# Decode out of the mLSTM loop, other PSUM banks, low parts on POOL, and a last tile in token order

## The chip, the cores and the metric

One core of one Trainium2 chip runs the whole program in one launch. The metric is device time in microseconds (us), the median of several runs. The engines are TensorE (PE, its weight loads as PEld), VectorE (DVE), ScalarE (ACT), GpSimd (POOL) and SyncE (SP, which issues most DMAs). DMA engines move data between HBM and SBUF; matmuls write to PSUM, which has eight banks here called `bk[0]` to `bk[7]`.

## The reference

Three layers follow one another, all with float32 results. The first is an mLSTM over 4 batches, 8 heads, 768 steps of width 40:

```
m_new = maximum(f[t] + m, i[t]);  fs = exp(f[t] + m - m_new);  is = exp(i[t] - m_new)
C = fs * C + is * outer(v[t], k[t]);   n = fs * n + is * k[t]
y[t] = sigmoid(o[t]) * (C @ q[t]) / maximum(abs(n . q[t]), 1)
```

Its result, 3072 tokens of width 320, goes to a mixture of 8 experts: `logits = x @ w_gate + modality_bias[modality]`, each token goes to the one expert with the largest logit, and gets `gate * (relu(x @ w1[e]) @ w2[e])`, where `gate` is the softmax weight of that expert and the inner width is 1024. The last layer is dense with inner width 2048: `h = x @ w_in; out = (h * cos(h)) @ w_out`.

## The kernel before, in words

All instructions stand in an order written out by hand (`manual_schedule`); each engine runs its own in that order and waits on semaphores for the others. A PSUM bank is one tile.

**mLSTM loop.** `for i in range(NT)`, 24 iterations; iteration i handles 128 steps (chunk c = i // 4) of batch i % 4. It issues `exps(i+1)` (ACT exponentials L427, POOL selections L436, POOL products), `scores(i)` (TensorE L466 and L474, VectorE products L480), `values(i-1)` (TensorE L493 into bank 6, L500, L508; VectorE L517 to L544; POOL division L546), loads for i+3 on SP, `spread_later(i+2)`, `logits(i-3)` (TensorE L570, VectorE L571) and `xpose(i-2)` (TensorE L557 into bank 2, ACT L559). Small VectorE work waits in a list `bg` of generators; `fill(n)` issues n of its operations at marked places, `drain()` all.

**Routing.** Every four iterations `route` chooses the expert of each token, and `rank_mm(c)` (L666 to L677) with `rank` (L692 on) counts its place among its expert's tokens; for chunks 0 to 3 the counts go to bank 6 (columns 64 on), for 4 to bank 7, for 5 to bank 4. `cnt` (L687) copies the totals after 16 and 20 iterations. `pick_first`, `early_slot` and `early_rows` choose the experts of slot 0 and 1 and find their rows with matmuls L815, whose result goes to bank 7 (slot 0) or bank 5; `gather` (L857, indirect DMA on POOL) then brings 256 rows of the tokens written so far into XS.

**Decode.** `w_in` and `w_out` of the last layer come as 64-bit words and are turned into float32 by `_decode`, 20 pieces of 128x512 or 128x640: ACT L1760, VectorE L1761, L1767, L1771, L1775, in four steps. Three pieces (`PIECES[:DA]`) are done in the mLSTM loop, two steps at the end of each iteration with i % 4 < 2 from 4 to 17, with loads on SP; the other 17 in slots 2 to 10, a step for each block, with loads on ACT's queue.

**Experts.** Tokens sorted by expert fill slots of 256 rows, s = 0 to 11, and seven shorter ones. A slot has 8 blocks f: `ffn1` (L976, 8 matmuls), `relu` (ACT L982 and VectorE L983, which makes the low part), `ffn2` of block f-2 (L997, 6 matmuls). Float32 precision comes from high and low parts: a weight is copied to a high part by ACT (L936, L945), and VectorE or POOL subtracts (`sub`, L927) to get the low part: `split_in(r1, f, d, eng, eng2)` for w1, `split_out` for w2. `xpose_b` makes the slot's input the same way (TensorE L877, ACT L881, VectorE L882). Ahead of slot 0, `first_slot` issues rank 4, then 14 operations of `bg`, then the low parts of blocks 1 and 2, then `xpose_b(0)`. `finish` scatters each result row to its place in `x2_d` (indirect DMA, index `cinv`), which `compact` computes so that unused rows are skipped; the row's number in the output is stored in its first column.

**Cosine stage.** 6 tiles of 512 rows of `x2_d`; 16 blocks each (`c_ffn1` L1651, `c_phase`, `c_cos`, `c_split`, `c_ffn2` L1683). The output rows are copied out of PSUM by VectorE (L1690) or ACT (L1692) in groups of 128 and scattered by POOL (L1003) to the rows given by `ids`.

Of the kernel before, what the change touches and what calls it, by code (L numbers as in the profile page):

```python
# [34 lines left out]
NTAB = NS + NU  # L35
EARLY = (16, 20)
DV = D + 1
MAGIC = 12582912.0
# [4 lines left out]
DU3 = 3  # L43
DA = 3
STEPS = (2, 2)

# [49 lines left out]
def kernel(  # L96
# [101 lines left out]

    F0 = 3

# [186 lines left out]
    Mc = many(ge2, B, "Mc", NP, DV)  # L387
    raw_t = [ge2.tile([128, 640, 2], U32, name=f"raw{i}") for i in range(2)]
    dtu_t = [ge2.tile([128, 640], U32, name=f"dtu{i}") for i in range(2)]
    for t_ in M[0:2]:  # L390
# [270 lines left out]
    def rank_mm(c):  # L661
        j0, n = c * B, B
        r = slice(j0, j0 + n)
        b_ = bk[(6, 7, 4)[max(c - NC + 3, 0)]]
        pk = b_[:, 64:64 + n * E]
        T_.matmul(out=pk, lhsT=trib[:, 0, :], rhs=oh[:, r].rearrange("p j e -> p (j e)"), start=True, stop=False)  # L666
        pk3 = pk.rearrange("p (j e) -> p j e", j=n)
        for j in range(n - 1):
            T_.matmul(
                out=pk3[:, j + 1:], lhsT=trib[:, 1, :],  # L670
                rhs=oh[:, j0 + j].unsqueeze(1).to_broadcast([128, n - 1 - j, E]), start=False, stop=False,
            )
# [9 lines left out]
    def rank_first(c, pk3):  # L682

        g = rank(c, pk3)
        next(g)
        if (c + 1) * B in EARLY:
            V.tensor_copy(out=cnt, in_=bk[6 if c < NC - 2 else 7][:, 128:128 + E])  # L687
        return g
# [151 lines left out]
    def early_rows(k):  # L840
        pv = bk[5 if k else 7][:, 0:4]
        slot_mm(k, EARLY[k], pv)
        with nc.allow_low_precision("whole numbers"):
            V.tensor_reduce(
                out=inv[:, 2 * k:2 * k + 2].unsqueeze(2), in_=pv.rearrange("p (a h) -> p h a", a=2), axis=AX.X,
                op=ALU.add,
            )
# [168 lines left out]
    def bstep(s, f):  # L1016
# [17 lines left out]
        if s > 2 or f > 1:  # L1034
            next(dec[0], None)
        if f == 4 and s + 1 < NS:
            fl[s + 1] = flag_regs(tab[s + 1:s + 2, 1:2])
# [24 lines left out]
    def weigh_later(c):  # L1062
        if c < SLOW:
            wt[c] = weights(c)
            bg.append(wt[c])
            return
        run(weights(c))
        wq.append(weigh(c))
        wt[c] = in_turn(rank_first(c, rank_mm(c)), rows_of(c))
        bg.append(wt[c])  # L1070

    dec_ops = _decode(nc, (raw_t, dtu_t), w_in, w_out, w_ir, None, PIECES[:DA])
    exps(0)
# [11 lines left out]
    for i in range(NT):  # L1085
# [8 lines left out]
        else:  # L1094
            exps(i + 1)
            if i >= 4 and i < NT - 1 and (i - 4) % B == B - 1 and (i - 4) // B >= SLOW:
                ex_exp((i - 4) // B)
            scores(i)
        if i == NT - 2:
            run(e0)  # L1100
            early_rows(0)
            gather(0)
        if i >= 1:
            values(i - 1)
# [27 lines left out]
        if i >= 3:  # L1132
            logits(i - 3)
        if i >= 2:
            xpose(i - 2)
        if i >= 8 and i % B == 0 and i // B - 2 < SLOW:
            c = i // B - 2
            bg.append(in_turn(rank_first(c, rank_mm(c)), rows_of(c)))
        if i >= 3 and (i - 3) % B == B - 1:
# [4 lines left out]
        if i >= 4 and i < NT - 1 and (i - 4) % B == B - 1:  # L1144
# [4 lines left out]
            weigh_later(c)  # L1149
            if i == EARLY[0] + 3:  # L1150
                pf = pick_first()
                bg.append(pf)
        if i >= 8 and i % B == 0 and i // B - 2 < SLOW:
# [7 lines left out]
        if i == EARLY[0] + 4:  # L1161
            load_w(0, 0)
        if i == 2:
            next(dec_ops)
        if B <= i < EARLY[0] + 2 and i % B < 2:
            for _ in range(STEPS[i % 2]):
                next(dec_ops, None)
        if i == NT - 2:
            for _ in dec_ops:
                pass  # L1170
            pe_.close()
# [7 lines left out]
    ex_exp(NC - 2)  # L1179
    split_in(w1r, 0, 0, G_, G_)  # L1180
    for f in (1, 2):
        split_in(w1r, f, f, V, V, (0,))
    run(weights(NC - 2))
# [5 lines left out]
    def first_slot():  # L1189
        rk_ = rank_first(NC - 2, rank_mm(NC - 2))  # L1190
        bg.extend([in_turn(pick_second(), early_slot(1, sc)), in_turn(rk_, rows_of(NC - 2))])
        fill(14)
        for f in (1, 2):
            split_in(w1r, f, f, V, V, (1,))
        for _ in xpose_b(0, (4, 1, 0)):
            fill(F0)
        for _ in range(2):
            next(we)
        split_out(w2r, 0, 0, V)

# [3 lines left out]
    split_in(w1r, 3, 3, V, V)  # L1204
    split_out(w2r, 1, 1, V)
    pl_.close()
# [71 lines left out]

    iv, pvs = small("iv", NL), small("pvs", NL)

    def slot_index():
# [4 lines left out]
        yield  # L1286
        V.scalar_tensor_tensor(out=inv[:, 4:], in0=pvs, scalar=-1.0, in1=iv, op0=ALU.add, op1=ALU.add)
        yield
# [37 lines left out]
    G_.memset(val[:, 0:4], 1.0)  # L1326
    pc = bk[3][:, 0:NH]

    def compact():
# [4 lines left out]
        yield  # L1334
        V.tensor_scalar(out=runs, in0=runs, scalar1=cst[:, C_P:C_P + 1], scalar2=4096.0, op0=ALU.add, op1=ALU.add)
        yield
        V.scalar_tensor_tensor(out=cinv, in0=val, scalar=-4096.0, in1=runs, op0=ALU.mult, op1=ALU.add)
        yield
# [23 lines left out]
    for k in range(2 * NF):  # L1362
        s, f = divmod(k, NF)
        ffn1(s, f)
        if k == 7:
            next(xgs[1])
        fill(2 if k in (0, 7) else 5)
        relu(s, f)
        if k == 7:
            next(xgs[1])  # L1370
        if k == 2:
            logits(NT - 2)
            xpose(NT - 1)
# [36 lines left out]
        if k == 5:  # L1410
            drain()
            we = weigh(NC - 1)
            bg += [halves()]
        if k >= 5:
# [7 lines left out]
        if NF - 3 <= k < 2 * NF - 3:  # L1422
            new_weights(1, k - NF + 3)
        if k == 8:
            drain()
# [4 lines left out]
        if k == 11:  # L1430
            drain()
            load_w(2, 0)
            V.tensor_scalar(out=val[:, 4:], in0=pvs, scalar1=0.0, scalar2=None, op0=ALU.is_gt)
        if k == 12:
            load_w(2, 1)
        if k == 13:
            T_.matmul(out=pc, lhsT=trib[:, 1, :], rhs=val, start=True, stop=True)
            bg += [compact(), out_rows()]
            xgs[2] = xpose_b(2)
# [25 lines left out]
    dtu_b = [rb.tile([128, 640], U32, name=f"dtu{i}") for i in range(2)]  # L1465
    dec[0] = _decode(nc, (raw_b, dtu_b), w_in, w_out, w_ir, w_or, PIECES[DA:], A)
    next(dec[0])
# [13 lines left out]
    def xpose_c(T, xs, xh, xl, banks):  # L1481
        G_.tensor_copy(out=ids[:, 4 * T:4 * T + 4], in_=xs[:, :, 3].bitcast(I32))
        A.activation(out=xs[:, :, 4 + DM:], in_=xs[:, :, 4 + 256:4 + DM], func=AF.Copy)
# [191 lines left out]
    def c_ffn2(T, *fs):  # L1675
        for j in range(TT):
# [10 lines left out]
            if fs[-1] == NFC - 1:  # L1687
# [3 lines left out]
                else:  # L1691
                    A.activation(out=os_, in_=po, func=AF.Copy)  # L1692
                scatter(out[:, :], ids[:, T * TT + j:T * TT + j + 1], os_, "out")

# [156 lines left out]
```

## Time and profile before

| what | value |
|---|---|
| median of 3 runs | 748.97 us (747.42 to 749.36) |
| profiled execution | 745.15 us, span 743.5 us, 16872 instructions |
| PE busy | 705.6 us (95%), 6132 matmuls |
| DVE busy | 527.9 us (71%) |
| ACT busy | 386.8 us (52%) |
| POOL busy | 214.9 us (29%) |
| HBM read, written | 84.58 MB, 12.14 MB |

The profile is taken from one execution; its time is the span plus what lies around it. Busy times are shares of the whole span, while the stages have different limits, so they are read by stretches. Matmul ends are modelled, so a busy PE is not PE at its peak.

### The profile page before, as it was taken

To read this page: it belongs to the slowest core of one execution; us is meant where nothing else is said; L and a number is where in the kernel's file an instruction comes from. 1 tells how busy PE (TensorE), PEld (TensorE's weight loads), DVE (VectorE), ACT (ScalarE), POOL (GpSimd) and SP (SyncE) were. 2 spreads that over 40 slices of the span, in tenths; PEclk is the share of its full clock that TensorE was granted. 3 is DMA by queue.
4 is the path that set the end of the run, shared out by engine and by line. 5 is a ranking of instruction groups with operands and counts; after the bars stand their busy time and mean duration, and the time that the engine had idled before them with its cause. 6 is when DMAs were issued, how large, how long until landed. Compare 5 with 4: busy or idle time off the path is not lost. (4 is left out here: it accounts for less than half of the span.)

```text
span 743.5 us, 16872 instructions
## 1 busy us (share of the span) xinstructions
PE 705.6 (95%) x6132; PEld 650.3 (87%) x6132; DVE 527.9 (71%) x1208; ACT 386.8 (52%) x910; POOL 214.9 (29%) x282
## 2 busy tenths in 40 slices
PE   8999898888999999999889999999999999999994
PEld 5898887878999999999868999999899999999994
DVE  7899988785456687772948866767667667667662
ACT  4666665442334555453735655555555555555551
POOL 7787774410542354411731002002002002001002
PEclk8999999999999999999999999999999999999998
DMA  7878787811544833505620101011011001000000
GB/s 187 229 201 237 210 226 226 240 37 38 172 110 119 260 117 108 147 25 178 206 75 1 31 6 36 1 36 36 1 36 36 1 1 36 0 1 19 19 1 35
DMA packets 45262, 68.42 MB, mean 92 GB/s; under 512 B 4846, under 2 KB 32944, under 8 KB 45168
## 3 DMA queue, kind: packets, MB, share of 16 engines
q1 hardware_dynamic: 37856, 45.16, 21.5%
q10 hardware_dynamic: 3664, 10.27, 4.7%
q0 software_dynamic: 3648, 11.82, 4.7%
q8 instruction: 49, 0.80, 0.5%
q14 instruction: 45, 0.37, 0.2%
HBM read 84.58 MB, written 12.14 MB: 130 GB/s over the span
## 5 line engine op out<-in xcount | busy, mean ns | idle before, releaser
L1663 ACT ACTIVATE w1r<-w1r 128x512 f32<-128x512 f32 x96 | 60.7, 633 | 104.2 <-DVE w1r L1658 97.9
L1665 DVE TENSOR_TENSOR w1r<-bk,w1r 128x512 f32<-128x512 f32 x96 | 66.3, 690 | 52.5 <-ACT w1r L1663 51.0
L1656 ACT ACTIVATE w1r<-bk,qtr 128x512 f32<-128x512 f32 x96 | 65.9, 686 | 57.5 <-PE bk L1651 54.9
L976 PE MATMUL bk<-XH,WIH 128*128 128x256 f32 x288 | 77.0, 296 | 2.9 <-DVE hl L983 1.6
L1657 DVE TENSOR_SCALAR w1r<-w1r 128x512 f32<-128x512 f32 x96 | 41.2, 429 | 52.5 <-ACT w1r L1656 50.7
L982 ACT ACTIVATE hh<-bk 128x256 fp32r<-128x256 f32 x96 | 36.6, 382 | 78.5 <-PE bk L976 59.3
L1683 PE MATMUL bk<-WOH,gh 128*128 128x320 f32 x228 | 71.0, 311 | 0.0
L1658 DVE TENSOR_TENSOR w1r<-w1r 128x512 f32<-128x512 f32 x96 | 68.3, 711 | 3.3
L1683 PE MATMUL bk<-WOH,gl 128*128 128x320 f32 x228 | 70.6, 310 | 0.0
L1683 PE MATMUL bk<-WOL,gh 128*128 128x320 f32 x228 | 70.4, 309 | 0.0
L983 DVE SCALAR_TENSOR_TENSOR hl<-bk,hh 128x256 fp32r<-128x256 f32 x96 | 40.0, 417 | 42.5 <-ACT hh L982 27.7
L1651 PE MATMUL bk<-XH,WIH 128*128 128x512 f32 x144 | 57.8, 401 | 4.3 <-issue 3.6
L997 PE MATMUL bk<-WOH,hl 128*128 128x320 f32 x192 | 59.7, 311 | 1.5 <-DVE hl L983 1.5
L976 PEld LDWEIGHTS bk<-XH,WIH 128*128 128x128 f32 x288 | 54.9, 191 | 5.8 <-DVEq L957 3.2
L997 PE MATMUL bk<-WOH,hh 128*128 128x320 f32 x192 | 59.7, 311 | 0.0
L1003 POOL DMA_INDIRECT x_d<-ys,cinv x26 | 30.7, 1182 | 99.8 <-ACTq L957 70.6
L997 PE MATMUL bk<-WOL,hh 128*128 128x320 f32 x192 | 59.4, 309 | 0.0
L1651 PE MATMUL bk<-XL,WIH 128*128 128x512 f32 x144 | 57.5, 399 | 0.0
L1651 PE MATMUL bk<-xh,WIH 128*128 128x512 f32 x144 | 56.5, 392 | 0.0
L1651 PE MATMUL bk<-xl,WIH 128*128 128x512 f32 x144 | 56.1, 389 | 0.0
L976 PE MATMUL bk<-XL,WIH 128*128 128x256 f32 x288 | 50.8, 285 | 2.5 <-DVE XL L882 2.5
L976 PE MATMUL bk<-XH,WIL 128*128 128x256 f32 x192 | 50.1, 283 | 0.0
(391 smaller groups left out, 1988.5 us busy)
## 6 DMA issues: line engine op xcount, KB each, us to landing
w2r<-in_w_dram SPq DMA_DIRECT2D x26, 640.0 KB
w1r<-in_w_dram SPq DMA_DIRECT2D x26, 512.0 KB
w1r<-in_w_dram SPq DMA_DIRECT2D x52, 128.0 KB
kvl<-in_kvn_dram SPq DMA_DIRECT2D x12, 484.0 KB
raw<-in_w_out_dram ACTq DMA_DIRECT2D x8, 640.0 KB
qkl<-in_qk_dram SPq DMA_DIRECT2D x24, 160.0 KB
x_d<-y SPq DMA_DIRECT2D x24, 160.0 KB
raw<-in_w_in_dram ACTq DMA_DIRECT2D x6, 512.0 KB
```

Of the source, the lines that this page charges most:

```text
L976: T_.matmul(out=ph, lhsT=a, rhs=x_, start=(n == 0), stop=(n == len(mms) - 1))
L982: A.activation(out=hh, in_=ph, func=AF.Relu)
L983: V.scalar_tensor_tensor(out=hl, in0=ph, scalar=0.0, in1=hh.bitcast(F32), op0=ALU.max, op1=ALU.subtract)
L997: T_.matmul(out=py(s, g), lhsT=a[:, gs], rhs=w_, start=(f == 0 and n == 0), stop=(f == NF - 1 and n == 2),)
L1003: r = G_.indirect_dma_start(out=dst, out_offset=bass.IndirectOffsetOnAxis(ap=idx, axis=0), in_=src, in_offset=None, bounds_check=NTOK - 1, ...
L1651: T_.matmul(out=ph, lhsT=a, rhs=x_, start=(n == 0), stop=(n == len(mms) - 1))
L1656: A.activation(out=v, in_=gp[T, f], func=AF.Identity, bias=qtr, scale=1.0 / (2 * math.pi))
L1657: V.tensor_scalar(out=kk, in0=v, scalar1=MAGIC, scalar2=MAGIC, op0=ALU.add, op1=ALU.subtract)
L1658: V.tensor_tensor(out=v, in0=v, in1=kk, op=ALU.subtract)
L1663: A.activation(out=v, in_=v, func=AF.Sin, scale=6.283185)
L1665: V.tensor_tensor(out=g, in0=gp.pop((T, f)), in1=v, op=ALU.mult)
L1683: T_.matmul(out=po, lhsT=a[:, js], rhs=w_, start=(f == 0 and n == 0), stop=(f == NFC - 1 and n == 2),)
```

## The change

Decode starts only behind slot 1: all 20 pieces are done from slot 2 on, with a second step in eleven blocks of slots 2 and 3, and the two pairs of buffers in the loop are gone. The rank counts of chunks 0 to 2 go to bank 2, columns 384 on, beside the transposes, and are issued ahead of `xpose`; those of chunk 3 go to bank 7 and are issued in iteration 20 behind the scores, together with `pick_first`. The first rows of slot 0 go to bank 2. The splits of w1r's blocks 0 to 2 are issued in the last loop iteration with the subtractions on POOL, those of w2r's blocks 0 and 1 have them on POOL too; `first_slot` takes 4 operations of `bg` in place of 14, then 2 behind each low part of the input (`F0`) in place of 3. In slots 0 and 1 `fill` follows `relu`, and `halves` starts at step 7 in place of 5. Tokens of the last chunk (from `TLATE` = 2560 on) are put in `x2_d` at their own numbers, the others are packed in front of them; so the last cosine tile is in token order and its output goes out by plain DMAs on SP.

```diff
-    F0 = 3
+    F0 = 2
...
-        b_ = bk[(6, 7, 4)[max(c - NC + 3, 0)]]
-        pk = b_[:, 64:64 + n * E]
+        b_, o = (bk[2], 384) if c < SLOW else (bk[7 if c < NC - 1 else 4], 64)
+        pk = b_[:, o:o + n * E]
...
-            V.tensor_copy(out=cnt, in_=bk[6 if c < NC - 2 else 7][:, 128:128 + E])
+            V.tensor_copy(out=cnt, in_=bk[7][:, 128:128 + E])
...
-        pv = bk[5 if k else 7][:, 0:4]
+        pv = bk[5][:, 0:4] if k else bk[2][:, 384:388]
...
         if s > 2 or f > 1:
             next(dec[0], None)
+        if s < 4 and s + f > 4:
+            next(dec[0], None)
...
         run(weights(c))
         wq.append(weigh(c))
-        wt[c] = in_turn(rank_first(c, rank_mm(c)), rows_of(c))
-        bg.append(wt[c])
-
-    dec_ops = _decode(nc, (raw_t, dtu_t), w_in, w_out, w_ir, None, PIECES[:DA])
...
+        if i == EARLY[0] + 4:
+            c, pf = SLOW, pick_first()
+            wt[c] = in_turn(rank_first(c, rank_mm(c)), rows_of(c))
+            bg += [wt[c], pf]
         if i == NT - 2:
             run(e0)
             early_rows(0)
             gather(0)
+        if i == NT - 1:
+            for f in range(3):
+                split_in(w1r, f, f, G_, G_)
         if i >= 1:
             values(i - 1)
...
+        c = i // B - 2
+        ranks = i >= 8 and i % B == 0 and c < SLOW
+        if ranks:
+            pk3 = rank_mm(c)
         if i >= 2:
             xpose(i - 2)
-        if i >= 8 and i % B == 0 and i // B - 2 < SLOW:
-            c = i // B - 2
-            bg.append(in_turn(rank_first(c, rank_mm(c)), rows_of(c)))
+        if ranks:
+            bg.append(in_turn(rank_first(c, pk3), rows_of(c)))
...
-        if i == 2:
-            next(dec_ops)
-        if B <= i < EARLY[0] + 2 and i % B < 2:
-            for _ in range(STEPS[i % 2]):
-                next(dec_ops, None)
...
-    split_in(w1r, 0, 0, G_, G_)
-    for f in (1, 2):
-        split_in(w1r, f, f, V, V, (0,))
...
-        fill(14)
-        for f in (1, 2):
-            split_in(w1r, f, f, V, V, (1,))
+        fill(4)
         for _ in xpose_b(0, (4, 1, 0)):
             fill(F0)
+        split_out(w2r, 0, 0, G_)
         for _ in range(2):
             next(we)
-        split_out(w2r, 0, 0, V)
...
-    split_out(w2r, 1, 1, V)
+    split_out(w2r, 1, 1, G_)
...
-        V.scalar_tensor_tensor(out=inv[:, 4:], in0=pvs, scalar=-1.0, in1=iv, op0=ALU.add, op1=ALU.add)
+        V.tensor_tensor(out=ivs[:, 4:], in0=pvs, in1=iv, op=ALU.add)
+        yield
+        V.tensor_scalar(out=inv[:, 4:], in0=ivs[:, 4:], scalar1=-1.0, scalar2=None, op0=ALU.add)
...
-        fill(2 if k in (0, 7) else 5)
         relu(s, f)
         if k == 7:
             next(xgs[1])
+        fill(5)
...
-            bg += [halves()]
...
+        if k == 7:
+            bg += [halves()]
...
-            V.tensor_scalar(out=val[:, 4:], in0=pvs, scalar1=0.0, scalar2=None, op0=ALU.is_gt)
+            V.tensor_scalar(out=val[:, 4:], in0=ivs[:, 4:], scalar1=TLATE + 0.5, scalar2=None, op0=ALU.is_lt)
...
             T_.matmul(out=pc, lhsT=trib[:, 1, :], rhs=val, start=True, stop=True)
+            T_.matmul(out=pw, lhsT=trib[:, 0, :], rhs=val, start=True, stop=True)
...
-    dec[0] = _decode(nc, (raw_b, dtu_b), w_in, w_out, w_ir, w_or, PIECES[DA:], A)
+    dec[0] = _decode(nc, (raw_b, dtu_b), w_in, w_out, w_ir, w_or, PIECES, A)
...
-                scatter(out[:, :], ids[:, T * TT + j:T * TT + j + 1], os_, "out")
+                if T < NTT - 1:
+                    scatter(out[:, :], ids[:, T * TT + j:T * TT + j + 1], os_, "out")
+                else:
+                    r = j * S + S - L
+                    nc.sync.dma_start(out=out[r:r + L, :], in_=os_)
```

The rest of the diff removes the constants and buffers of the first decode, computes `cinv` in six operations in place of four, and leaves out the copy of `ids` for the last tile.

## Rows read from the trace of the kernel before

**Rows 1.** Windows: stretch, length, busy us (instructions) of PE, PEld, DVE, ACT, POOL.

```profile
60.00:80.00 20.00, 18.60 (x406) 17.51 (x406) 19.17 (x64) 12.95 (x46) 15.09 (x23) 1.00 0.87 228
...
200.00:220.00 20.00, 19.54 (x150) 19.03 (x149) 12.09 (x24) 7.08 (x19) 11.07 (x13) 1.00 0.46 132
```

**Rows 2.** Timeline of PE, score matmuls: start, length, engine, line, operation.

```profile
48.58 1.06 PE L466 MATMUL bk<-qkl 128*128 128x128 f32 x8
53.28 1.06 PE L466 MATMUL bk<-qk 128*128 128x128 f32 x8
...
107.78 1.06 PE L466 MATMUL bk<-qkl 128*128 128x128 f32 x8
...
126.16 1.06 PE L466 MATMUL bk<-qkb 128*128 128x128 f32 x8
```

**Rows 3.** Waits, 0 to 145 us: who waited for whom, total, times, longest.

```profile
PE bk L493 <- DVE tot L692: 1.8, 3, 0.6
...
PE bk L666 <- DVE Ml L517: 1.7, 1, 1.7
...
PE bk L493 <- DVE cnt L687: 1.5, 1, 1.5
...
PE bk L815 <- DVE lg L571: 1.1, 1, 1.1
```

**Rows 4.** Groups by line, 0 to 200 us, decode on DVE: busy us, mean ns.

```profile
L1767 DVE SCALAR_TENSOR_TENSOR dtu<-raw,dtu 128x512 uint32<-128x512 uint32 x3 | 3.3, 1094 | 0.1
...
L1775 DVE SCALAR_TENSOR_TENSOR w_ir<-dtu,dtu 128x512 f32<-128x512 f32 x3 | 3.1, 1025 | 0.3
...
L1771 DVE SCALAR_TENSOR_TENSOR dtu<-raw,dtu 128x512 uint32<-128x512 uint32 x3 | 2.0, 683 | 0.0
L1761 DVE TENSOR_SCALAR dtu<-raw 128x512 uint32<-128x512 uint32 (+1 forms) x4 | 2.0, 504 | 0.4 <-DMA raw<-in_w_out_dram 0.4
```

**Rows 5.** Timeline of DVE behind the first-row matmuls.

```profile
137.56 0.50 DVE L522 TENSOR_TENSOR hq<-bk,eG 128x328 f32<-128x328 f32 x1 [2.65 <-issue]
```

**Rows 6.** Windows at low clock; the clock is the third number from the right.

```profile
152.00:156.00 4.00, 4.00 (x29) 3.78 (x29) 3.90 (x16) 2.69 (x7) 0.91 (x2) 0.57 0.00 0
134.50:138.70 4.20, 4.20 (x59) 4.16 (x58) 1.23 (x4) 0.00 (x0) 3.28 (x4) 0.61 0.71 198
```

**Rows 7.** Waits of PE, 140 to 200 us.

```profile
PE bk L976 <- DVE XL L882: 2.5, 3, 1.3
...
PE bk L997 <- DVE hl L983: 1.5, 2, 1.2
...
PE bk L877 <- DMA XS<-x_d,inv: 0.9, 2, 0.6
```

**Rows 8.** Windows of line L927 alone: busy us of DVE and POOL.

```profile
148.00:152.90 4.90, 1.64 (x5) 0.00 (x0) 0.96 0.23 80
144.00:148.00 4.00, 0.00 (x0) 1.14 (x2) 1.00 0.86 248
```

**Rows 9.** Timelines of POOL and DVE: one small DVE operation, twice.

```profile
121.23 0.72 POOL L546 TENSOR_TENSOR y<-y,den 128x320 f32<-128x320 f32 x1 [4.26 <-DVE gate L614]
121.25 0.73 DVE L616 TENSOR_SCALAR gate<-gate 128x4 f32<-128x4 f32 x1
...
165.35 0.16 DVE L616 TENSOR_SCALAR gate<-gate 128x4 f32<-128x4 f32 x1
```

**Rows 10.** Timeline and windows: the end, and a store of y on SP.

```profile
734.23 0.49 DVE L1690 COPY os__9533<-bk 128x320 f32<-128x320 f32 x1 [2.15 <-PE bk L1683]
735.34 0.98 POOL L1003 DMA_INDIRECT out_dram<-os__9533,ids  x1 [0.30 <-issue]
737.00:737.25 0.25, 0.00 (x0) 0.00 (x0) 0.00 (x0) 0.00 (x0) 0.00 (x0) 0.50 0.94 348
...
166.42 2.42 SPq L625 DMA_DIRECT2D x_d<-y  x4
167.25:167.50 0.25, 0.25 (x4) 0.25 (x3) 0.25 (x1) 0.25 (x2) 0.00 (x0) 1.00 0.88 323
```

More of the change, by code (lines that the diff above doesn't have):

```diff
@@ L36 @@
 EARLY = (16, 20)
+TLATE = EARLY[1] * 128
 DV = D + 1
@@ L43 @@
 DU3 = 3
-DA = 3
-STEPS = (2, 2)
 PIECES = [p for q in range(4) for p in (q, 4 + q, 8 + q, 12 + 2 * q, 13 + 2 * q)]
@@ L387 @@
     Mc = many(ge2, B, "Mc", NP, DV)
-    raw_t = [ge2.tile([128, 640, 2], U32, name=f"raw{i}") for i in range(2)]
-    dtu_t = [ge2.tile([128, 640], U32, name=f"dtu{i}") for i in range(2)]
     for t_ in M[0:2]:
@@ L1149 @@
             weigh_later(c)
-            if i == EARLY[0] + 3:
-                pf = pick_first()
-                bg.append(pf)
         if i >= 8 and i % B == 0 and i // B - 2 < SLOW:
@@ L1162 @@
             load_w(0, 0)
-        if i == 2:
-            next(dec_ops)
-        if B <= i < EARLY[0] + 2 and i % B < 2:
-            for _ in range(STEPS[i % 2]):
-                next(dec_ops, None)
         if i == NT - 2:
-            for _ in dec_ops:
-                pass
             pe_.close()
@@ L1279 @@
     iv, pvs = small("iv", NL), small("pvs", NL)
+    ivs = small("ivs", NH)
+    V.memset(ivs[:, 0:4], 0.0)
     def slot_index():
@@ L1326 @@
     G_.memset(val[:, 0:4], 1.0)
-    pc = bk[3][:, 0:NH]
+    pc, pw = bk[3][:, 0:NH], bk[3][:, 64:64 + NH]
     def compact():
@@ L1334, in compact @@
         yield
-        V.tensor_scalar(out=runs, in0=runs, scalar1=cst[:, C_P:C_P + 1], scalar2=4096.0, op0=ALU.add, op1=ALU.add)
+        V.tensor_tensor(out=runs, in0=runs, in1=pw, op=ALU.add)
         yield
-        V.scalar_tensor_tensor(out=cinv, in0=val, scalar=-4096.0, in1=runs, op0=ALU.mult, op1=ALU.add)
+        V.scalar_tensor_tensor(out=runs, in0=runs, scalar=1.0, in1=ivs, op0=ALU.add, op1=ALU.subtract)
+        yield
+        V.tensor_tensor(out=runs, in0=runs, in1=val, op=ALU.mult)
+        yield
+        V.scalar_tensor_tensor(out=cinv, in0=runs, scalar=-1.0, in1=ivs, op0=ALU.add, op1=ALU.add)
         yield
@@ L1481, in xpose_c @@
     def xpose_c(T, xs, xh, xl, banks):
-        G_.tensor_copy(out=ids[:, 4 * T:4 * T + 4], in_=xs[:, :, 3].bitcast(I32))
+        if T < NT // 4 - 1:
+            G_.tensor_copy(out=ids[:, 4 * T:4 * T + 4], in_=xs[:, :, 3].bitcast(I32))
         A.activation(out=xs[:, :, 4 + DM:], in_=xs[:, :, 4 + 256:4 + DM], func=AF.Copy)
```

## The prediction

> **What bounds the kernel now.** I read the busy time by stretches of 20 us first, then the timeline of TensorE and of VectorE in the stretches where TensorE has gaps, then who waited for whom. There are three kinds of stretch. From 200 us on TensorE is the engine that never stops: in 200 to 220 it is busy 19.54 of 20 us and VectorE 12.09 [rows 1]; the same holds through the cosine stage, which the change leaves alone but for its last tile. In the mLSTM loop (20 to 135 us) VectorE is as full as TensorE: in 60 to 80 us VectorE 19.17, TensorE 18.60 [rows 1]. Between the two, around slot 0 (140 to 180 us), TensorE stops again and again for VectorE.
>
> The reader can take the floor of one mLSTM iteration from the first score matmul (L466) of one to that of the next: 48.58 to 53.28 is 4.70 us, with TensorE busy throughout. Ten iterations from 53.28 to 107.78 took 54.50, so 7.5 us more than ten floors; the three from 107.78 to 126.16 took 18.38, 4.3 more than three [rows 2]. What ends TensorE's own waits in the loop is named in rows 3: the value matmuls L493 waited 1.8 us in three waits for `tot` L692 and 1.5 for `cnt` L687 (rank counts in bank 6, which L493 is about to write), the rank matmul L666 1.7 for `Ml` L517 (the same bank), and the first-row matmuls L815 1.1 for `lg` L571, which reads other columns of bank 7: the wait is for a bank, not for the columns.
>
> **The change, part by part.**
>
> Decode leaves the mLSTM. Three pieces go, four VectorE operations each: L1767 3.3 us, L1771 2.0, L1775 3.1, and three of L1761 at 0.50, 1.5 together: 9.9 us [rows 4], and three ScalarE operations and three 0.5 MB loads on SP's queue, which wait there between the loads of q, k and v. VectorE loses 9.9 us in a stretch where it has almost no idle time, but TensorE's floor stops the gain: the iteration of 4.70 us just quoted runs beside full VectorE work. Two of the three pieces (6.6 us, issued at the ends of iterations 8, 9, 12 and 13; 53.28 begins iteration 8) and the three rank stalls (1.8) lie in the ten iterations whose excess is 7.5. The ends for this part with the rank stalls are 1.8 (the decode was hidden, only the stalls go) and 7.5 (all ten run at the floor). I take 5.5, nearer the upper end, because VectorE with 19.17 of 20 us is the nearest row: a queue that long makes its late results late for everyone.
>
> Ranks and first rows in other banks. Ranks 0 to 2 go to bank 2, beside the transposes, and are issued ahead of them; rank 3 goes to bank 7 and is issued behind the scores of iteration 20 instead of at the end of 19. The three waits of 1.8 are in the sum above. In the iterations 18 to 20 the 1.7 and 1.5 go [rows 3], at most 3.2 of an excess of 4.3; at least nothing, because VectorE has the same work there, now with the rank behind the scores' two multiplications, and TensorE may still wait at L666 for the last read of bank 7. I take 1.3. L815 in bank 2 no longer waits for L571: 1.1. Behind that wait the granted clock was 0.61 over 134.5 to 138.7, that is mostly the lower level, 1.2 GHz; at 2.4 GHz throughout it would have taken (1 - 0.61) x 4.2 = 1.6 less [rows 6]. VectorE stood 2.65 us idle in front of L522 for it [rows 5]. So up to 2.7 is there to be won. But what comes next is the input of slot 0, and TensorE already waits 0.9 us for it in two waits of L877 for the gathered XS [rows 7]. Loads of 2.8 MB and the gather share the DMA engines at that point, and the gather is issued behind POOL's selection, which the bank does not touch. What TensorE gains ahead of it, it mostly waits away there: I take 0.5 (ends 0 and 2.7).
>
> Low parts near slot 0. The subtractions of w1r's blocks 1 and 2 (two each) and of w2r's blocks 0 and 1 go from VectorE to POOL, those of w1r in the last loop iteration; 14 queued small operations ahead of slot 0's own low parts (XL L882) become 4. Five of the six that leave VectorE took 1.64 us, the sixth the same as the fifth, some 0.4: 2.0 [rows 8]. TensorE waited 2.5 us in three waits for XL [rows 7], and ran slot 0's next matmuls at a clock of 0.57 over 152 to 156, which is (1 - 0.57) x 4.0 = 1.7 us lost [rows 6]. The most is 4.2. But the small operations aren't gone, they now run between the first blocks of slot 0, where VectorE is the late engine, so what lasts is its shorter work plus a little of the clock: 2.4. The least is 0.3, if POOL holds VectorE up (next paragraph). On ScalarE three copies L936 now stand ahead of the next xT copy and wait for the first half of w1r; they have room before TensorE needs that xT. If that cover fails, they cost their own length, which the ends hold.
>
> POOL's price. Two of these subtractions already ran on POOL: 1.14 us for the two [rows 8], so four more cost 2.3 there, and the two wider ones perhaps 1.5 (an estimate from the same row by width). A VectorE operation that meets a POOL operation is stretched: L616 took 0.73 us while POOL ran L546 (0.72), and 0.16 at 165 us with POOL idle [rows 9]. If VectorE met each of the six new ones for its whole length, it would lose 3.8 us. The Trainium skill (SBUF — State Buffer, Who interferes with whom) says that the port pair which the two engines share is an exclusive lock held for a whole instruction, and the loser blocks entirely; by that the sum below would be some 8 instead of 12, and row L616 agrees with it. I don't take it in full, since most of what VectorE has then reads PSUM.
>
> Fill behind relu. In slots 0 and 1 the queued operations now follow the low part of the activation (L983), and `halves` starts two steps later. TensorE waited 1.5 us for L983 in two waits [rows 7], which stood behind five operations of `halves`. I take 1.2 (ends 0.5 and 1.5): what was put off is still due before the first-row matmuls of slot 2.
>
> The last tile. Now the last copy ends at 734.23 + 0.49 = 734.72, POOL issues its scatter at 735.34 behind three others, and the last output bytes move in the slice from 737.00 [rows 10], ending about 737.3. On SP the store of y, the same 160 KB, is issued from 166.42 and its bytes run in the slice from 167.25 [rows 10]: some 0.8 us, and 0.5 for the bytes. The last tile would end at 734.8 + 1.3 = 736.1, a gain of 1.2. The 6 us from there to the end of the span stay. Ends 0 (completion is slower on that queue) and 1.6.
>
> Back in slots 2 and 3. Eleven more decode steps stand in two slots where VectorE is 40% idle [rows 1]: nothing, as long as that cover holds; without it up to 9.9 us. As a bound for small collisions I keep 1.5. One more operation ahead of gather(2), two in the compaction, one more matmul: each about as short as L616 alone [rows 9], beside full TensorE, nothing.
>
> Sum: 5.5 + 1.3 + 0.5 + 2.4 + 1.2 + 1.2 = 12.1 us; all low ends with the 1.5 give 1.1, all high ends 20.7. The profiled execution took 745.15 (span 743.5): 733.0 after. It lies 3.8 under the median of the runs, 748.97, and on that scale the forecast is 736.9, said as 737.
>
> **The rivals.**
>
> VectorE's relief is not passed on. The iterations stay bound by TensorE and by the chain through ScalarE, as in the 4.70 us; only stalls with a name go: 1.8, 0.5, 0.3 to 1, 1.2 and the tail 1.2, about 5.5: 743.5. For it: decode beside the floor. Against it: 7.5 us of excess that TensorE's named waits explain by 1.8 only.
>
> The shared port. VectorE is held up by POOL's subtractions for 3.8 us around slot 0, where it is the late engine: 740.8. For it: L616. Against it: they run while TensorE waits for XS.
>
> All bubbles close. The loop runs at its floor to the end and the clock stays at its upper level at both places: 18 to 20.7, about 730. Against it: XS.
>
> Slower. In slots 2 and 3 each added decode operation stands ahead of an L983 for which TensorE waits: 9.9 us. It decides from the point where the rest gives less than that; with the first part and slot 0's at their low ends (VectorE's time is of no use anywhere else either) the rest gives 12.1 - 3.7 - 2.1 = 6.3, and the time is 748.97 + 3.6 = 752.6. For it: VectorE's operations are the same wherever they run. Against it: 7.9 us idle in 20 there, and activations are wanted only two steps after they are made.
>
> The change without effect, because both stretches are bound by DMA landings: 748.
>
> **How the numbers follow.** Forecast 0.52, relief not passed on 0.18, port 0.10, all bubbles 0.10, slower 0.06, no effect 0.04. Two runs can be told apart from 0.3%, 2.2 us. The first four are all faster by more; I leave 0.04 of them to the band within it: faster 0.86, same 0.08, slower 0.06. The range goes from 729.5 (all bubbles, nearly all of it) to 745.5 (relief not passed on, with 2 us less than its sum) and leaves out no effect, slower and the outer tails.
>
> **What would show it.** Iterations 9, 10, 13 and 14 near 4.7 us and no wait of L493 for `tot` or `cnt`; VectorE idle of more than 1 us in 60 to 80; the L815 wait gone and a longer wait of L877 for XS instead; XL within 1.5 us of the first L976 of slot 0; a granted clock near 1 in the 4 us after it; no TensorE wait near `halves`; last output bytes about 1.4 us after the last copy; slots 2 and 3 as long as before. The forecast is wrong if the mLSTM takes as long with VectorE idle, if POOL's subtractions double VectorE's small operations, or if slot 2 grows by more than 2 us.

## The result, and the profile after

The changed kernel takes 740.12 us (median of 12 runs, 737.0 to 745.73), the kernel before 748.49 in the same comparison (12 runs, 744.9 to 749.36): a ratio of 0.9899, 95% interval 0.9879 to 0.9918, 1.0% faster. A second comparison gave 738.77 against 743.68, 0.9916 (0.9879 to 0.9953). The forecast was 737.0 with a range of 729.5 to 745.5, so time and direction came out. Its sum did not: two terms were wrong by much, in opposite directions, and that they partly cancel is luck.

The profiled executions took 745.15 and 739.58 us, spans 743.5 and 737.9: 5.6 us of the 8.4 between the medians. The one before lies 3.3 under its median, and where the other executions spend that isn't seen. What follows explains the 5.6.

In the loop the changes arrived. PE's score matmuls at the starts of iterations 8, 18 and 21 (start, length, engine, line), the answer to [rows 2]:

```profile
53.52 0.39 PE L464 MATMUL bk<-qk 128*128 128x128 f32 x2
...
101.73 0.42 PE L464 MATMUL bk<-qkl 128*128 128x128 f32 x2
...
120.35 0.50 PE L464 MATMUL bk<-qkb 128*128 128x128 f32 x3
```

Ten iterations take 48.21 us, 54.50 before: nine of them 4.69 to 4.88, one 5.37. The next three take 18.62, 18.38 before: nothing was gained there. Two windows answer to [rows 1] (length, then busy us of PE, PEld, DVE, ACT, POOL):

```profile
60.00:80.00 20.00, 20.00 (x450) 19.25 (x446) 18.95 (x67) 14.29 (x53) 16.28 (x26) 1.00 0.83 229
200.00:220.00 20.00, 17.36 (x120) 15.33 (x118) 13.71 (x26) 8.09 (x20) 7.58 (x8) 1.00 0.42 131
```

TensorE is full in the first now. In the second, where it had 19.54 of 20 us, it has 17.36: the new loss. TensorE's waits from 20 to 147 us (who waited for whom, total, times, longest) answer to [rows 3] and the XS row of [rows 7]:

```profile
PE bk L664 <- DVE lg L569: 2.3, 2, 1.4
...
PE bk L875 <- DMA XS<-x_d,inv: 1.0, 1, 1.0
```

The waits for `tot`, `cnt` and `Ml` are gone, and so is that of the first-row matmuls. The rank matmul L664 now waits in bank 7 for the logits, as the first-row matmuls did before.

A mark that every slot has is SP's issue of the next weights in its first block (L887, before L889). With SP's load of the first cosine tile (L1481, before L1479) it shows how the lead came and went:

| mark | before | after | lead |
|---|---|---|---|
| start of iteration 18 | 107.78 | 101.73 | 6.1 |
| start of iteration 23 | 138.70 | 130.30 | 8.4 |
| first-row matmuls behind slot 0's start | 159.71 | 149.63 | 10.1 |
| weights of slot 2 | 186.81 | 175.84 | 11.0 |
| slot 2, first block | 195.75 | 186.17 | 9.6 |
| slot 4, first block | 228.90 | 224.47 | 4.4 |
| slot 5, first block | 244.44 | 240.02 | 4.4 |
| slot 6, first block | 260.98 | 258.53 | 2.5 |
| first cosine tile's load | 347.07 | 345.82 | 1.3 |
| last matmul starts | 733.88 | 733.80 | 0.1 |
| end of the span | 743.5 | 737.9 | 5.6 |

So 11 us were won ahead of slot 2, all were lost again by the last matmul, and the 5.6 that remain come from behind it. The tail, answering to [rows 10] (last copy, last transfer, and two windows with DMA share and GB/s at the right):

```profile
734.15 0.49 DVE L1693 COPY os__9528<-bk 128x320 f32<-128x320 f32 x1 [2.15 <-PE bk L1686]
734.67 0.33 SPq L1700 DMA_DIRECT2D out_dram<-os__9528  x1
...
735.50:736.00 0.50, 0.00 (x0) 0.00 (x0) 0.00 (x0) 0.00 (x0) 0.00 (x0) 1.00 0.90 323
736.00:736.50 0.50, 0.00 (x0) 0.00 (x0) 0.00 (x0) 0.00 (x0) 0.00 (x0) 1.00 0.02 5
```

The last bytes move at about 736.1, 1.4 us behind the end of the last copy (734.64), where the forecast had 736.1. But the span ends 1.8 us later, where it ended 6.0 us behind the last bytes before (737.5 to 743.5).

Where slots 2 and 3 lose, ScalarE's and VectorE's timeline around 200 us shows. L1767 is ScalarE's first operation of a decode piece, L1782 VectorE's last; both use the buffer `u` (`dtu` in the rows):

```profile
199.25 0.68 DVE L1782 SCALAR_TENSOR_TENSOR w_ir<-dtu,dtu 128x512 f32<-128x512 f32 x1
200.02 0.68 ACT L1767 ACTIVATE dtu<-raw 128x512 f32<-128x512 f32 x1 [2.65 <-issue]
...
201.25 0.38 ACT L980 ACTIVATE hh<-bk 128x256 fp32r<-128x256 f32 x1
201.68 0.42 PE L995 MATMUL bk<-WOH,hh 128*128 128x320 f32 x1 [1.44 <-ACTq L955]
```

ScalarE stands 2.65 us in front of L1767. The releaser is given as "issue", but L1767 starts 0.09 us after L1782 of the piece before has ended (199.93), and about so it does at the three other long waits (211.58, 216.93, 222.16). The next `hh` stands behind it, and TensorE waits. In slot 5 another wait of ScalarE has grown, from 0.5 us (L945) before. ScalarE's waits from 186 to 262 us:

```profile
ACT dtu L1767 <- issue: 9.8, 4, 3.0
...
ACT WOH L943 <- DMA w2r<-in_w_dram: 2.3, 1, 2.3
```

### The profile page after: what moved, and what is told of

The parts are those of the page before. It is cut to its first block, busy times and chain, and to the rows that moved or that the text cites. A ratio compares the mean times of both kernels' runs of the same rounds, so it can differ in the third digit from the quotient of the medians.

```text
span 737.9 us, 16878 instructions
## 1 busy us (share of the span) xinstructions
PE 707.3 (96%) x6133; PEld 650.8 (88%) x6133; DVE 524.8 (71%) x1206; ACT 388.2 (53%) x910; POOL 212.2 (29%) x283
```

## The experiments

Each was compared with the kernel before on the same chip; ratios are to it. "Slots 2+3" is from the mark of slot 2 to that of slot 4, "slot 5" from that of slot 5 to that of slot 6, "loop" iterations 8 to 17.

| kernel | ratio (95%) | loop | slots 2+3 | slot 5 |
|---|---|---|---|---|
| before | 1 | 54.50 | 33.15 | 16.54 |
| changed | 0.9899 (0.9879 to 0.9918) | 48.21 | 38.30 | 18.51 |
| changed again | 0.9916 (0.9879 to 0.9953) | 48.89 | 37.07 | 18.25 |
| last tile scattered | 0.998 (0.9953 to 1.0007) | 47.94 | 36.72 | 21.73 |
| last tile on POOL's queue | 0.996 (0.9935 to 0.9985) | 49.44 | 39.27 | 18.24 |
| second u | 0.9924 (0.9901 to 0.9947) | 49.23 | 33.45 | 23.48 |
| pairs in step | 0.994 (0.9918 to 0.9962) | 48.87 | 36.76 | 18.73 |
| u in place | 0.9896 (0.9856 to 0.9937) | 49.35 | 34.33 | 21.89 |
| u in place, again | 0.9908 (0.9878 to 0.9938) | 50.00 | 33.90 | 21.54 |
| u in place, raw between weights | 0.9874 (0.9856 to 0.9893) | 49.67 | 38.25 | 16.54 |
| decode in loop | 0.9834 (0.9811 to 0.9856) | 52.83 | 32.11 | 16.53 |
| decode in loop, rank 3 in bank 2 | 0.9878 (0.9836 to 0.9919) | 52.74 | 32.21 | 16.54 |
| decode in loop, u in place | 0.983 (0.9814 to 0.9846) | 52.81 | 34.60 | 16.55 |
| low parts on VectorE | 0.9912 (0.9884 to 0.994) | 49.32 | 37.64 | 18.30 |

**Last tile scattered.**

```diff
-                if T < NTT - 1:
-                    scatter(out[:, :], ids[:, T * TT + j:T * TT + j + 1], os_, "out")
-                else:
-                    nc.sync.dma_start(out=out[r:r + L, :], in_=os_)
+                scatter(out[:, :], ids[:, T * TT + j:T * TT + j + 1], os_, "out")
...
```

> The changed kernel with its last cosine tile as before: slot order, row ids copied, output by POOL's indirect transfer; everything else of the change stays. In the profiles the last matmul ends at 734.19 before and 734.11 after, so of the 5.6 us between the two spans 5.5 lie behind it. Theory A (the end of the program waits some 6 us behind the last bytes of POOL's indirect queue, but 1.9 behind those of SP's plain transfers): 740.1 + 5.5 = 745.6, and again some 6 us between the last output bytes and the end of the span. Rival (the prediction's term: only issue and landing differ, 1.2 us, and the rest of the 5.5 is chance of the two profiled executions): 741.3, with 2 us behind the last bytes.

745.47 us, ratio 0.998: no longer to be told from the kernel before. The last bytes move until about 737.9 and the span ends at 743.9, 6.0 us behind. Theory A holds.

**Last tile on POOL's queue.**

```diff
-                    nc.sync.dma_start(out=out[r:r + L, :], in_=os_)
+                    G_.dma_start(out=out[r:r + L, :], in_=os_)
```

> The changed kernel with the last tile's four plain output transfers issued by POOL instead of SP; the token order stays. If POOL's queue is what makes the end late (6.0 us from the last output bytes to the end of the span, 1.85 with SP): some 6 us again, and 739 + 4.5 = 743 to 745, ratio 0.996 to 0.999. If the indirect form is: 2 us, time and ratio as the changed kernel (0.9899 and 0.9916 in two comparisons).

744.79 us, 0.996: nearly all of the tail's gain is gone, though the transfers are plain and in token order. Its last issue and the windows that hold the last bytes:

```profile
736.43 0.54 POOL L1700 DMA_DIRECT2D out_dram<-os__9528  x1 [0.84 <-DVE os__9528 L1693]
...
737.50:738.00 0.50, 0.00 (x0) 0.00 (x0) 0.00 (x0) 0.00 (x0) 0.00 (x0) 1.00 0.89 328
738.00:738.50 0.50, 0.00 (x0) 0.00 (x0) 0.00 (x0) 0.00 (x0) 0.00 (x0) 1.00 0.01 0
```

The span ends at 744.1, again 6.0 us behind the last bytes (738.1). From the start of the last matmul to the end it took 8.8 us, 4.1 in the changed kernel and 9.6 before. What counts is that the last transfers are issued by POOL and go through its queue, not their indirect form; engine and queue are not told apart.

**Decode in loop.** The first three pieces back at their old places, no doubled steps in the slots.

```diff
+        if i == 2:
+            next(dec_ops)
+        if B <= i < EARLY[0] + 2 and i % B < 2:
+            for _ in range(STEPS[i % 2]):
+                next(dec_ops, None)
...
-        if s < 4 and s + f > 4:
-            next(dec[0], None)
```

> The changed kernel with the first three decode pieces back in the mLSTM loop at their old places, and no doubled steps in slots 2 and 3; banks, fill, low parts and last tile as changed. If the loop's gain of 6.3 us in iterations 8 to 17 came from the decode and lasted to the end: 740.1 + 4 to 6 = 744 to 746. If what the loop gains is lost again in slots 2 and 3 (their loads show the lead fall from 9.5 to 4.4 us there): loop 4 to 6 us longer, slots 2 and 3 4 to 5 us shorter, 739.5 to 742. If the loop's gain came from the rank banks alone: loop as in the changed kernel, slots 2 and 3 shorter, 735 to 737.

The second case, and stronger than expected: 732.81 us, 0.9834, faster than the changed kernel. The starts of its iterations 8 and 18:

```profile
53.45 0.50 PE L468 MATMUL bk<-qk 128*128 128x128 f32 x3
...
106.28 0.39 PE L468 MATMUL bk<-qkl 128*128 128x128 f32 x2
```

52.83 us, and 52.74 and 52.81 in the two other kernels of this kind: the decode costs 4.6 us in the loop (52.83 - 48.21; 2.8 to 4.9 over all kernels without it there), and the rank banks with the order of the ranks won 1.7 (54.50 - 52.83). From slot 2 on it loses nothing to the kernel before; slots 2+3 are even 1 us shorter. So the decode's move, taken alone, made the kernel slower. VectorE's busy time in these ten iterations is 50.58 us here and 44.75 in the changed kernel, 5.8 less, near the 4.6 that the loop gains. But three ScalarE operations and three loads moved with it, and the runs do not separate them.

**Second u.**

```diff
-        hi, lo, t, u = raw[:, :n, 1], raw[:, :n, 0], t_[:, :n], u_[:, :n]
+        hi, lo, t, u = raw[:, :n, 1], raw[:, :n, 0], t_[:, :n], us_[n_ % len(us_)][:, :n]
...
-        ys = ys_t[h % 4]
+        ys = ys_t[h % 3]
```

> The changed kernel with a second buffer u for ScalarE's copy L1767 in the decode, used in turn (to make room, three row buffers of the slot output instead of four). Theory B (in slots 2 and 3 L1767 waits in ScalarE's queue, four times 2.1 to 3.0 us, until VectorE has done L1782 of the piece before, which read the same u; XH and hh stand behind it and TensorE waits for them): these four waits go, slots 2 and 3 take 2 to 5 us less than the 38.3 us from load to load (186.17 to 224.47), and the time falls by 2 to 4.5: 735.5 to 738. Rival C (it is VectorE's added work in these slots, whatever waits for what): slots and time as in the changed kernel, 740.1 within 1. Rival D (slots 2 and 3 get shorter, but the start of the cosine stage is set by something else, as the 2.2 us of lead at the end of the branches became 0.5): slots shorter, time 739 to 740.

Slots 2+3 fall to 33.45 us as theory B says, but the time stays, 740.32. Two other stretches took it back. Three row buffers cost a wait in front of slot 2 (ScalarE's L1010 2.9 us for the scatter of a row buffer), and slot 5 grew to 23.48, with 5.7 us of ScalarE waiting for w2r:

```profile
252.78 0.47 ACT L943 ACTIVATE WOH<-w2r 128x320 fp32r<-128x320 f32 x1 [5.65 <-DMA w2r<-in_w_dram]
```

**Pairs in step.**

```diff
-        if s < 4 and s + f > 4:
+        if s == 2 and f > 1 or s == 3 and f > 3:
             next(dec[0], None)
```

> The changed kernel with the doubled decode steps placed so that no block holds the last step of a piece together with the first of the next (doubled in all blocks of slot 2 from its third and in the last four of slot 3; ten extra steps, not eleven). VectorE's work in the two slots is nearly the same. Theory B: L1782 is issued a block ahead of the next L1767, so the four waits of 2.1 to 3.0 us shrink to under 1, and the time falls by 2 to 4.5 us: 735.5 to 738. Rival C (VectorE's volume): 740 within 1. Rival D as before: slots 2 and 3 shorter, time 739 to 740.

In time a miss: 740.63, slots 2+3 36.76. The four long waits did go, as theory B says; no wait of L1767 is over 1.3 us. But TensorE now waits in slot 2 for the gathered input of the next slot, which waited 0.7 us in the second profile of the changed kernel (TensorE's waits from 186 to 224 us):

```profile
PE bk L875 <- DMA XS<-x_d,inv: 2.6, 1, 2.6
```

This kernel doubles from the third block of slot 2 on, one block earlier than the changed one, and so issues a raw piece earlier. The kernel that does so too, below, shows the same wait.

**U in place.** L1767 writes to the piece's place in the weights, L1782 works there.

```diff
-        A.activation(out=u.bitcast(F32), in_=hi.bitcast(F32), func=AF.Abs)
+        A.activation(out=dst, in_=hi.bitcast(F32), func=AF.Abs)
...
-            out=dst, in0=u.bitcast(F32), scalar=3.4332275390625e-05, in1=t.bitcast(F32), op0=ALU.is_ge, op1=ALU.mult
+            out=dst, in0=dst, scalar=3.4332275390625e-05, in1=t.bitcast(F32), op0=ALU.is_ge, op1=ALU.mult
```

> The changed kernel with the decode's u written straight to the piece's place in the weights, where L1782 then works in place: no buffer u that two pieces share, and no other edit (the second-buffer kernel had also three row buffers for four, and lost 2.9 us waiting for one). Theory B (L1767 stood behind L1782 of the piece before): slots 2 and 3 take 33 to 35 us instead of 38.3, the start of slot 2 keeps its lead, and the slots from 186 to 224 us gain 3.5 to 5. Theory E (the weight transfer of slot 5 is late because raw pieces are issued in the same blocks f=0 and f=4 as the halves of the weights, w2r waits of 2.3 to 5.7 us against 0.5): the loss in slot 5 stays or grows, 18.5 to 23 us. Together 735 to 739. Rival C (VectorE's volume): slots 2 and 3 unchanged, 740.

Beside it ran the changed kernel once more.

> The changed kernel once more, as the measure for the kernels beside it and as a second profile. If the loss behind the lead is part of the kernel and not chance of one execution: slots 2 and 3 from load to load again 37 to 39 us (before 33.15), slot 5 over 17.5 (before 16.54), last matmul within 1.5 us of the one of the kernel before, some 2 us between last output bytes and end; time 738 to 741.

That held: 738.77 us, slots 2+3 37.07, slot 5 18.25, and the last matmul starts at 734.09. Its trace names the releaser of L1767's long waits:

```profile
ACT dtu L1767 <- DVE w_ir L1782: 4.8, 3, 2.6
...
ACT dtu L1767 <- DVE w_or L1782: 4.0, 2, 3.0
```

With u in place it is 737.38 us, slots 2+3 take 34.33, and what is left of L1767's waits (186 to 262 us) is:

```profile
ACT w_or L1767 <- ACTq L955: 0.9, 3, 0.3
ACT w_ir L1767 <- ACTq L955: 0.9, 3, 0.3
```

1.8 us. VectorE has as many operations as in the changed kernel, so it is not their volume (rival C). Of the 2.7 to 4.0 us won there, slot 5 took back 3.4 to 3.6 (ScalarE waits 4.1 for w2r).

**U in place, again.** The same kernel, beside it on the same chip.

> As the kernel with u in place, beside it on the same chip, for the spread of the slot-5 loss: if it is set by the program, slot 5 takes the same time within 1 us in both profiles; if by chance of the transfers, it differs by more. Time within 1 us of the other.

737.73 us, slots 2+3 33.90, slot 5 21.54: the loss in slot 5 belongs to the program.

**U in place, raw between weights.**

```diff
-        if s < 4 and s + f > 4:
+        if s < 4 and f > 1:
             next(dec[0], None)
```

> The kernel with u in place, and one doubled decode step more (slots 2 and 3 both from their third block on): from slot 4 on each raw piece is issued in blocks 3 and 7 instead of 0 and 4, where the two halves of the weights are issued. Theory E (the raw pieces hold up w2r, for which ScalarE's L943 waits in slot 5): slot 5 takes 16.5 to 17.5 us from load to load, where u in place alone took 21.9 and 21.5, and the time is 4 to 5 us less: 0.983 to 0.985 of the kernel before, against 0.990 and 0.991. Rival (the transfers of slot 5 are bound by their bytes, in any order): slot 5 over 20 us, ratio 0.990.

Theory E holds for slot 5: 16.54 us. The piece is issued between the halves of the weights (SP's L887 begins each half), and ScalarE's wait for w2r is back at 0.5:

```profile
241.21 0.40 SPq L887 DMA_DIRECT2D w1r<-in_w_dram  x1
...
244.76 0.35 ACTq L1742 DMA_DIRECT2D raw<-in_w_in_dram  x1
...
246.96 0.37 SPq L887 DMA_DIRECT2D w1r<-in_w_dram  x1
```

The time misses its expectation: 737.28, 0.9874 for 0.983 to 0.985. Slot 2, where the doubling begins a block earlier as in pairs in step, takes 19.9 us (16.7 with u in place), and TensorE waits there for the next slot's input. The raw piece (L1744) is issued at 189.19, between the two gathers (188.38 and 189.74); with u in place it was 190.18, behind both (187.49 and 188.86):

```profile
195.72 0.33 PE L875 MATMUL bk<-cst,XS 128*128 128x128 f32 x1 [2.67 <-DMA XS<-x_d,inv]
```

**Decode in loop, rank 3 in bank 2.**

```diff
-        b_, o = (bk[2], 384) if c < SLOW else (bk[7 if c < NC - 1 else 4], 64)
+        b_, o = (bk[2], 384) if c <= SLOW else (bk[7 if c < NC - 1 else 4], 64)
...
```

> The changed kernel with the decode's first three pieces in the loop again, and rank 3 in bank 2 like ranks 0 to 2, so that L664 no longer waits for lg in bank 7 at iteration 20 (1.36 us in the changed kernel's profile). If that wait is what holds iterations 19 and 20 (5.76 and 8.14 us): 1 to 1.5 us less than decode in the loop alone (732.8, ratio 0.9834): 731 to 732. Rival (VectorE's and ScalarE's chain at the early selection holds them: the gate and P are late whatever the bank): no change, 732.8 within 0.7.

The rival, if anything worse: ratio 0.9878, with intervals that touch. L668's wait for the logits (1.4 us) is gone, but the wait for `P` (ScalarE's L429) grew from 1.4 to 2.8, so TensorE stands about as long, now in one piece (its waits from 110 to 138 us, then iteration 21, with the granted clock third from the right):

```profile
PE bk L262 <- ACT P L429: 2.8, 1, 2.8
```

```profile
125.98:132.48 6.50, 6.50 (x88) 6.26 (x88) 4.08 (x18) 3.59 (x12) 2.34 (x3) 0.62 0.86 263
```

Iterations 18 to 21 take 25.64 us, 22.96 in decode in loop with rank 3 in bank 7. The chain of the early selection holds them with either bank, and what this kernel loses on top goes with the clock: behind the one long wait it was 0.62, mostly the lower level of 1.2 GHz, and the iteration took 6.50 us; decode in loop had 1.00 and 4.59 us there (124.65 to 129.24).

**Decode in loop, u in place.**

> The changed kernel with the decode's first three pieces back in the loop (as in decode in loop, ratio 0.9834) and u written in place. With single decode steps L1767 waited for L1782 only 1 us at a time, so little is to be won: loop, slots 2 and 3 and slot 5 as in decode in loop (52.8, 32.1, 16.5 us), ratio 0.982 to 0.985. Against u in place with the raw pieces between the weights: if decode in the loop costs 4.6 us there and the added steps in slots 2 and 3 cost 2 to 3 us without the shared u, this one is 1 to 3 us slower than that; if the added steps still cost more elsewhere, it is faster.

735.03 us, 0.983, as decode in loop without it: two comparisons, one ratio. Loop and slot 5 are as expected, slots 2+3 are not (34.60, with a wait of L879 of 1.4 us for XL). It is the last case: with the added steps, freed of the waits for `u` and w2r, it was 0.9874 on the same chip, and slower.

**Low parts on VectorE.**

```diff
-                split_in(w1r, f, f, G_, G_)
+                split_in(w1r, f, f, *((V, V) if f else (G_, G_)))
...
-        split_out(w2r, 0, 0, G_)
+        split_out(w2r, 0, 0, V)
...
```

> The changed kernel with the six low parts near slot 0 on VectorE instead of POOL, at the places where the change put them. The change's part from the first matmul of slot 0 to the first-row matmuls took 8.2 to 9.0 us in all kernels with the subtractions on POOL, 11.88 before; from the start of iteration 23 to the first matmul of slot 0 10.9 to 12.0 us, 9.13 before. The prediction (VectorE is the late engine, 2.0 us of work leave it): the two stretches together take 1 to 3 us more than the changed kernel's 19.3 and 20.8. The shared-port rival (POOL's subtractions stretch VectorE's operations by up to their length): they take 1 to 2 us less, above all the first.

From the start of iteration 23 to the first-row matmuls it took 20.84 us. The nine other profiles with the decode in the slots took 19.3 to 20.8, the kernel before 21.01. Neither the prediction nor the rival: the engine of these six operations can't be seen in the time. The windows of this stretch, of the changed kernel and then of this one:

```profile
130.30:149.60 19.30, 17.10 (x219) 15.47 (x217) 18.00 (x73) 12.09 (x31) 9.04 (x14) 0.91 0.55 166
```

```profile
131.55:152.39 20.84, 18.50 (x220) 16.81 (x218) 19.21 (x85) 12.52 (x31) 4.95 (x8) 0.84 0.53 157
```

The whole windows cannot be set against each other as they stand: the longer one holds 17 subtractions (L925) on VectorE, the other 8, and of these nine only six are the moved ones, which take some 2.4 us here. It can be seen operation by operation. One small operation of VectorE in the changed kernel, beside POOL's subtraction, and then in this one, with POOL idle:

```profile
141.20 0.88 POOL L925 TENSOR_TENSOR WOL<-w2r,WOH 128x320 fp32r<-128x320 f32 x1 [2.83 <-ACT WOH L943]
141.45 0.66 DVE L721 SCALAR_TENSOR_TENSOR e<-sc,m,cst 128x8 f32<-128x8 f32 x1
```

```profile
143.14 0.22 DVE L721 SCALAR_TENSOR_TENSOR e<-sc,m,cst 128x8 f32<-128x8 f32 x1
```

With L587 (0.41 for 0.19), L589 (1.15 for 0.27) and one L925 (0.97 for 0.27), the VectorE operations that meet a subtraction on POOL (those of block 0, on POOL in every kernel, included) are 2.2 us longer than here; the seven other profiles of kernels with the same lines have 2.8 to 3.3. So about as much came back to VectorE as was taken off it. The Trainium skill (SBUF — State Buffer, Who interferes with whom) has the two engines share a port pair that one of them holds alone; the trace agrees, with 2.2 to 3.3 us where the rival had 3.8. TensorE's waits for `XL`, 2.5 us before [rows 7], are gone with either engine, so POOL was not needed for that; fewer queued operations ahead of `XL` is the part of the change made for it, and was not tried alone.

## Why the prediction was right, and where it was wrong

Profiled, its steps came to this (second profile of the changed kernel in brackets):

| step | forecast | measured |
|---|---|---|
| loop, iterations 8 to 17 | 5.5 | 6.3 (5.6) |
| iterations 18 to 20 | 1.3 | -0.2 (0) |
| first-row bank and low parts, iteration 21 to the first-row matmuls | 2.9 | 4.3 (2.9) |
| fill behind relu, to the next first-row matmuls | 1.2 | 1.1 (1.8) |
| lead by slot 2's weights | 10.9 | 11.0 (9.1) |
| decode in slots 2 and 3, to the first cosine tile's load | 0, a loss of 1.5 at most | -9.7 (-8.1) |
| last tile | 1.2 | 5.5 |

- **Loop.** Right in size and in its parts: 4.6 for the decode and 1.7 for the banks, where the named rank stalls were 1.8. Iterations 9, 10, 13 and 14 took 4.69 us each, as named ahead. Decode in loop shows that the decode cost this time; that it did so through VectorE's full queue, as the prediction says, fits VectorE's busy time but is not shown apart from ScalarE's part and the loads.
- **Iterations 18 to 20.** Wrong: the two waits went, others took their place, and rank 3 in bank 2 won nothing either.
- **First-row bank, low parts.** The sum held, its parts did not. Iterations 21 and 22 gained 2.6 us (12.54 to 9.95), near the 2.7 that was called the most for the bank: the wait of 1.1 is gone, and the clock behind it is 1.00 (next point). The bank was not tried alone. Then L664 waits 0.9 for the logits and L875 1.0 for XS, so the gain is partly waited away, as said. Of the low parts, the waits for `XL` went, but with either engine. That VectorE's work gets shorter did not come: POOL's subtractions stretched its operations by about what they took off. The reason for not taking the port in full, that VectorE mostly reads PSUM then, does not fit: L587, L589, L721 and L925 read SBUF.
- **Fill.** Right in size and by its wait: TensorE's waits for `hl` around slots 0 and 1 fell from 1.5 us [rows 7] to 0.3.
- **Clock.** Behind the first-row matmuls it stayed up, 1.00, the upper level of 2.4 GHz, where it was 0.61 in [rows 6]:

```profile
126.50:130.30 3.80, 3.80 (x76) 3.72 (x72) 2.03 (x8) 1.40 (x6) 2.90 (x4) 1.00 0.78 232
```

Around slot 0's first matmul (141.48) it did not, against the sign named ahead: it was 0.53, mostly the lower level of 1.2 GHz, from 140.3 to 143.9 us (0.57 in [rows 6]), with TensorE 7.50 of 9.70 us busy ahead of it (130.3 to 140).

- **Last tile.** The step that failed is "the 6 us from there to the end of the span stay". The last bytes were placed rightly; those 6 us come with the last transfers issued by POOL, and 4.2 of them go when SP issues them. I had taken them for the program's own end.
- **Back in slots 2 and 3.** The step that failed is "nothing, as long as that cover holds". I counted VectorE's idle time, and it was there. What the added steps cost was something else. The 9.7 us were lost in four places: 5.2 in slots 2 and 3, 2.0 in slot 5, 1.4 in front of slot 2, 1.2 in slots 6 to 11. ScalarE's first operation of a piece waits for VectorE's last of the piece before, through one buffer, and doubled steps put both in one block: u in place gets back 2.7 to 4.4 us in slots 2+3 (38.30 and 37.07 to 34.33 and 33.90). And eleven more steps shift all later pieces to the blocks in which the weights are issued: raw between weights gets back 5 us in slot 5 against u in place. What it loses in slot 2 instead, for XS, comes with a raw piece issued ahead of the gather, and is likely the same thing at another place; moving that piece alone was not tried. Why slot 5 loses 2 us in some kernels and 5 to 7 in others stays open. The loss in slots 6 to 11 (2.2 in the second profile) and that in front of slot 2 (0.3 in the second) were not tested.
- **Rivals.** The one with the price of 9.9 us without cover came in, but mostly by another path: it is ScalarE that TensorE waits for. That 9.7 us were lost is no confirmation of its price: in slots 2 and 3, where it put them, it was 5.2 (3.9 in the second profile). With the rest as large as it was, that does not end slower than before. The shared port came in too, with most of its price, but the time did not show it. Most of the chance lay on the forecast, whose working assumed that it would not come. The time lay in the range, near the forecast, because the tail gave 4.3 us more than forecast and the slots 9.7 less; that is luck.
- **What would have shown it.** The sign named ahead against the forecast was slot 2 longer by more than 2 us. It took 18.97 us for 16.19 before, and 17.73 in the second profile; so the sign came true once, and slots 2 and 3 together were longer by 5.2 and 3.9. POOL's subtractions also made small operations of VectorE longer (L721 three times as long), another sign named ahead.

One gap stands outside all this. Between the last short block and the first cosine matmul TensorE waits 3.6 to 4.0 us in the kernel before and in all experiments, while instructions are being loaded (0.05 MB on that queue from 371 to 378 us in the changed kernel). In the first profile of the changed kernel it was 5.28, which took 1.7 us of the lead; the second had 3.74. It doesn't belong to the change.

The best version found is the changed kernel with the decode left in the loop: 732.81 and 735.03 us in its two forms, 0.983 of the kernel before.

## What to carry to other kernels

Work moved under an engine's idle time is free only if its waits are too: look which buffer ties its first operation to its last, what stands behind that operation on its queue, and beside which transfers its own loads now land. Measure a move alone before it is judged in company: here a gain of 5.5 us at the tail covered a loss. When the end of a program is looked at, read the distance from the last bytes to the end of the span, and through which queue those bytes went.

## What the runs showed of the hardware

- From the last output bytes to the end of the span it took 6.0 us in all three kernels whose last transfers went through POOL's queue (indirect twice, plain once), and 1.8 where SP issued them (both profiles of the changed kernel). The Trainium skill (DMA: Bandwidth & Descriptors, Anatomy of one DMA — SWDGE (gpsimd) path) puts the fixed cost of a DMA from GpSimd at about 2 us, mostly the receipt of the last write; the 6 us at the end of this program are more, and the measurement decides.
- In this program, where a bank is one tile, a matmul waits for a read of other columns of its PSUM bank: L664, which writes columns 64 and up of bank 7, waited 1.4 and 0.9 us for the logits' read of it, as L815 did before [rows 3]. The wait is a semaphore of the program; no run tries the chip without it.
- With a 0.5 MB piece issued within 0.6 us of each half of the weights (in pairs in step 1.6 us behind the first), w2r kept ScalarE waiting 1.8 to 5.7 us. Issued between the halves it was 0.5, and 1.1 and 2.0 in two kernels with the decode in the loop; that of 2.0 lies in slot 6, which took 16.6 us there and 15.5 before. The DMA engines of the changed kernel were busy 0.92 to 1.06 of the time there (242 to 252 us, in windows of 2 us), at up to 399 GB/s.
- A VectorE operation on SBUF that meets a subtraction on POOL takes longer: L721 0.66 us beside it and 0.22 without, 0.56 to 0.91 in the kernels with these subtractions on POOL.
